# Attention and a feed-forward product on one core: row maximum and shift of the scores in one VectorE operation that works in place, and another order at the start

## The chip, the cores and the metric

One core of a Trainium2 chip runs the whole program. The metric is the device time of one execution in microseconds (us), given as the median over runs. TensorE (PE in the profile) does the matrix products and transposes, its weight loads are counted apart (PEld), VectorE is DVE, ScalarE is ACT, GpSimd is POOL, and SyncE (SP) issues every DMA.

## The reference

Queries, keys and values have 8 batches, 12 heads, 448 positions and 64 features. `g_q` and `g_k` are vectors of 64.

```
q_n, k_n = rmsnorm(q, g_q), rmsnorm(k, g_k)      # x / sqrt(mean(x*x) + 1e-6) * g
scores = q_n @ k_n.T / sqrt(64)
scores = scores - max(scores, axis=-1)
attn = exp(scores); attn = attn / (sum(attn, axis=-1) + 1e-9)
x = (attn @ v), heads side by side               # 3584 rows of 768
h = x @ w_in                                      # 768 x 2048
y = (h * cos(h)) @ w_out                          # 2048 x 768
```

The two weight matrices arrive as 64-bit floats.

## The kernel before

Two heads of one batch make a pair; there are 48 pairs, numbered u, six to a batch. The operands of the products are split into a rounded high part and a low rest (`hi` against `l` or `lo` in the names), and a product is summed up from passes over these parts.

What is done for a pair falls into two functions of the planner. `prepare(u)` loads the squares' input `sd`, squares it on ACT (L280), sums it on DVE (L283), and turns the sums into `r` = mean square to the power of -1/2 on POOL (`st_pow`, L291). `r` has 14 columns: 0 to 6 belong to the query rows, 7 to 13 to the key rows. The key factors go out to DRAM (`st_store`, L294) and come back spread over partitions as `rkb` (`rk_load`, L299); POOL multiplies the keys by them (`k_norm`, L309), ACT makes `khi` (L312) and POOL `kl` (L316). The queries are only multiplied by the gains (`q_scale`, L323), and split into `qhi` (L326) and `ql` (L330). The values are split on POOL (`v_high` L339, `v_low` L343).

`attend(u)` works on seven score tiles `S` of 128 query rows by 448 keys, each in one bank of PSUM; three such banks go round. `score` (L357) fills two tiles at a time, then one. `rowmax` (L363, one for each tile) takes the row maximum, `shift` (L368, one for each `score` call, so four for a pair) multiplies it by minus the query factor, and `expo` (L373) takes the exponential on ACT with the query factor as its scale and the shift as its bias, and sums the rows in the same pass. `sm` is the small tile of maxima, shifts and sums. The probabilities are transposed on TensorE four key blocks after another into one PSUM tile `PT` (L400), copied as `hi` on ACT (L407) and `lo` on DVE (L415, L417), and multiplied with the values into `O` (L427). The transposed row sums pass through the same tile (L402, once for a pair). After six pairs the batch is ready for the first product `ph` with `w_in` (L470 to L472), whose pieces stand between those of the next batches' attention. The weights `w_in` are decoded from 64 bits by four DVE operations (L208 to L216) and one on ACT (L214), split on ACT (L226) and POOL (L231). `w_out` goes the same way later. When all attention is done, a second part of the program does the cosine and the second product `y` (L541 to L543).

The order on every engine is set by a list scheduler at build time, `Plan`: each step is added with an engine, a cost in us, a due time, and the data that it reads and writes; at each free moment of an engine the step with the earliest due time among those that are ready is put next. `base(u)` is the due time of pair u, `SPLIT` the distance from the last pair of a batch to its first product. `SIGNAL` is added when a step waits for another engine, and `LEAD` on top of it when the waiting engine is TensorE. On the chip each engine then runs its list strictly in that order, and waits where the data is not there.

```
    SIGNAL = 0.16
    LEAD = 0.3
    ...
        return 30.0 + (PER0 * u if u < NP else PER0 * NP + PER * (u - NP))
```

Of the kernel before, what the change touches and what calls it, by code (L numbers as in the profile page):

```python
# [10 lines left out]
F32 = mybir.dt.float32  # L11
# [3 lines left out]
ALU = mybir.AluOpType  # L15
AX = mybir.AxisListType
# [11 lines left out]
class Plan:  # L28
# [9 lines left out]
    def __init__(self, rings):  # L38
        self.rings = rings
        self.parts = []  # L40
        self.start = []
        self.writer = {}
        self.readers = {}
        self.users = {}

    def add(self, eng, cost, due, fn, *args, r=(), w=(), land=0.0, start=0.0):
# [18 lines left out]
        self.start.append(start)  # L65

    def order(self):
# [21 lines left out]
        while True:  # L89
# [35 lines left out]
def tile_attention_moe(  # L125
# [11 lines left out]
    nc = tc.nc  # L137
# [4 lines left out]
    NVC = 5  # L142
    NCC = 6
# [38 lines left out]
    def g_fold():  # L182
# [7 lines left out]
        "sd": 1, "r": 5, "rkb": 1, "kd": 1, "kl": 2, "khi": 2, "qd": 1, "ql": 2, "qhi": 2, "vd": 1, "vs": 2, "S": 3, "sm": 3, "P": 12,  # L190
# [98 lines left out]
    def st_pow(u):  # L289
        r = pair[u]["r"]  # L290
        nc.gpsimd.tensor_tensor(r, r, nhalf.broadcast_to([128, 14]), ALU.pow)  # L291
# [52 lines left out]


    def score(u, j):
# [5 lines left out]
        for t in tiles:  # L352
            d["S", t] = ps_s.tile([128, 512], F32, tag="S", name=f"S{u}_{t}")
# [8 lines left out]
    def rowmax(u, t):  # L362
        nc.vector.reduce_max(pair[u]["sm"][:, 0, t : t + 1], pair[u]["S", t][:, :S], axis=AX.X)  # L363

    def shift(u, j):
        sm, r = pair[u]["sm"], pair[u]["r"]
        c = slice(3, 4) if j == 3 else slice(j, j + 5, 4)
        nc.vector.scalar_tensor_tensor(sm[:, 1, c], sm[:, 0, c], -1.0, r[:, c], op0=ALU.mult, op1=ALU.mult)  # L368

    def expo(u, t):  # L370
# [4 lines left out]
            bias=sm[:, 1, t : t + 1], scale=d["r"][:, t : t + 1], accum_out=sm[:, 2, t : t + 1],  # L375
# [187 lines left out]
    SPLIT = 56.0  # L563
# [3 lines left out]
    def base(u):  # L567
        return 30.0 + (PER0 * u if u < NP else PER0 * NP + PER * (u - NP))
# [33 lines left out]
    def prepare(u):  # L602
# [8 lines left out]
        add(POOL, 2.58, D0 - 34, st_pow, u, w=r)  # L611
        add(SP, ISS, D0 - 30, st_store, u, r=r, w=[("rkd", u)], land=LAND)
        add(SP, 2 * ISS, D0 - 26, rk_load, u, r=[("rkd", u)], w=[("rkb", u)], land=6.5)
# [3 lines left out]
        add(POOL, 0.8, D0 - 16, q_scale, u, r=[("gsc", 0)], w=qd)  # L617
        add(ACT, 0.6, D0 - 10, q_high, u, r=qd, w=qhi)
        add(POOL, 1.33, D0 - 8, q_low, u, r=qd + qhi, w=[("ql", u)])
        for hh in range(2):  # L620
            vd, vs = [("vd", 2 * u + hh)], [("vs", u, hh)]
            add(SP, ISS, D0 - 12 + 6 * hh, v_load, u, hh, w=vd, land=LAND)
            add(POOL, 0.56, D0 + 6 * hh, v_high, u, hh, r=vd, w=vs)
            add(POOL, 0.91, D0 + 2 + 6 * hh, v_low, u, hh, r=vd, w=vs)

    def attend(u):
        D0 = base(u)
        b, cc = divmod(u, NP)
        step = 4.0
        for j in range(4):  # L630
            tiles = (3,) if j == 3 else (j, j + 4)
            keys = [("S", 7 * u + 2 * j + n) for n in range(len(tiles))]
            dj = D0 + step * j
            add(PE, 0.88 if j < 3 else 0.62, dj, score, u, j,
                r=[("qhi", u), ("ql", u), ("khi", u), ("kl", u)], w=keys)
            for t, key in zip(tiles, keys):
                add(DVE, 0.61, dj + 1, rowmax, u, t, r=[key], w=[("sm", u, 0, t)])
            add(DVE, 0.25, dj + 1, shift, u, j, r=[("r", u)] + [("sm", u, 0, t) for t in tiles], w=[("sm", u, 1, j)])
            for n, (t, key) in enumerate(zip(tiles, keys)):
                add(ACT, 0.94, dj + 2, expo, u, t, r=[key, ("r", u), ("sm", u, 1, j)],  # L640
# [4 lines left out]
        for kc in range(4):  # L645
            dk = D1 + 4 * kc
            for hh, tiles in ((0, (0, 1, 2, 3)), (1, (4, 5, 6))):
# [8 lines left out]
                add(PE, 0.47 if hh == 0 else 0.36 + 0.11 * turn, dk, transp, u, kc, tiles, turn, r=r, w=w)  # L656
# [11 lines left out]
            for hh in range(2):  # L668
                n, m = 8 * u + 2 * kc + hh, 6 * u + 2 * kc + hh
                r = [[("hi", n), ("lo", m)], [("hi", n), ("lo", m)], [("lo", m)], [("hi", n), ("hi", n - 2)]][kc]  # L670
                add(PE, 0.21 if kc == 2 else 0.41, dk + 4, av, u, kc, hh, r=[("vs", u, hh)] + r, w=[("O", u, hh)])
# [126 lines left out]
```

## Time and profile before

| | us |
|---|---|
| median of 3 runs | 1604.09 |
| lowest and highest run | 1601.24 and 1608.01 |
| the profiled execution | 1605.41 |
| span of its profile | 1603.6 |
| busy: PE, PEld | 1483.6, 1250.6 |
| busy: DVE, ACT, POOL | 1081.9, 909.1, 880.9 |
| mean granted TensorE clock | 0.974 of full speed |

Busy times are sums over the span. What a stage is bound by is read from windows of the span, since the attention (from 30 us to some 1060 us) and the second product (the rest) have different limits. TensorE's matrix products overlap each other, so that one shows some 0.37 us where they start 0.20 us apart.

### The profile page before, as it was taken

The numbers are of one execution on the slowest core, as the hardware profiler recorded it, in microseconds if no ns is written. First come the engines' busy times: TensorE is split into PE (matmuls) and PEld (weight loads), VectorE is DVE, ScalarE is ACT, GpSimd is POOL, SyncE is SP. The second block draws the span as 40 slices with busy tenths as digits, with TensorE's granted clock in tenths as the row PEclk, the third lists the DMA queues.
The fourth block names the chain that finished last, engine by engine and source line by source line (L and its number), as shares of the span: only waits on it lengthen the run. The fifth ranks groups of instructions, "written<-read, shape, count | busy, mean of one in ns | idle before, by whom it ended". The sixth has DMA issues, their size and how long they took to land.

```text
span 1603.6 us, 22333 instructions
## 1 busy us (share of the span) xinstructions
PE 1483.6 (93%) x7680; PEld 1250.6 (78%) x7680; DVE 1081.9 (67%) x1723; ACT 909.1 (57%) x1786; POOL 880.9 (55%) x726
## 2 busy tenths in 40 slices
PE   0777889989999999999999999999999999999999
PEld 0455677778778877877777877879999999999998
DVE  5665899968777777787777776525266666666661
ACT  3556676667666677766677666634243444444432
POOL 7655767876475666576556564223245445444441
PEclk9877899999999999999999999999999999999999
DMA  5333662355445545545445543129422232322220
GB/s 168 106 91 117 193 212 92 110 149 166 147 148 158 160 145 163 158 132 161 133 136 168 152 148 92 54 83 353 138 92 69 93 104 60 102 92 81 81 81 35
DMA packets 118433, 205.24 MB, mean 128 GB/s; under 512 B 19680, under 2 KB 97840, under 8 KB 118320
## 3 DMA queue, kind: packets, MB, share of 16 engines
q1 hardware_dynamic: 118320, 203.82, 40.8%
q8 instruction: 60, 0.98, 0.3%
q14 instruction: 53, 0.43, 0.1%
HBM read 150.47 MB, written 53.30 MB: 127 GB/s over the span
## 4 chain that ended last, share of the span: by engine, by line
PE 60%; DVE 7%; ACT 4%; issue 2%; POOL 1%; DMA 0%; SPq 0%; ACTq 0%; POOLq 0%; DVEq 0%
PE y L541 10%; PE y L543 10%; PE y L542 10%; PE ph L470 6%; PE ph L471 6%; PE ph L472 6%; PE O L427 5%; PE PT L400 4%; PE S L357 4%; ACT hi L407 2%; DVE sm L363 1%; DVE lo L415 1%; ACT P L373 1%; DVE xf L442 1%; ACT xf L437 1%
## 5 line engine op out<-in xcount | busy, mean ns | idle before, releaser
L470 PE MATMUL ph<-xs,wi 128*128 128x448 f32 x768 | 300.5, 391 | 14.7 <-ACT he L482 14.7
L407 ACT CAST hi<-PT 128x448 fp32r<-128x448 f32 x384 | 187.9, 535 | 172.6 <-PE PT L400 72.5
L373 ACT ACTIVATE P<-S,sm,r 128x448 f32<-128x448 f32 x336 | 243.7, 732 | 73.8 <-DVE sm L368 72.7
L471 PE MATMUL ph<-xs,wi 128*128 128x448 f32 x768 | 284.0, 370 | 1.4 <-POOL xs L456 1.4
L472 PE MATMUL ph<-xs,wi 128*128 128x448 f32 x768 | 282.5, 368 | 0.0
L541 PE MATMUL y<-g,wo 128*128 128x448 f32 x768 | 281.1, 366 | 0.0
L542 PE MATMUL y<-g,wo 128*128 128x448 f32 x768 | 280.6, 365 | 0.0
L543 PE MATMUL y<-g,wo 128*128 128x448 f32 x768 | 280.6, 365 | 0.0
L525 POOL TENSOR_TENSOR g<-r,g 128x896 fp32r<-128x896 f32 x64 | 139.6, 2182 | 183.2 <-ACT g L527 183.2
L415 DVE TENSOR_TENSOR lo<-PT,hi 128x448 fp32r<-128x448 f32 x288 | 166.1, 616 | 95.4 <-ACT hi L407 91.9
L363 DVE TENSOR_REDUCE sm<-S 128x1 f32<-128x448 f32 x336 | 196.0, 613 | 43.1 <-PE S L357 42.3
L400 PE MATMUL PT<-ident,P 128*128 128x128 f32 x1344 | 194.0, 288 | 1.4 <-ACT P L373 1.4
L400 PEld LDWEIGHTS PT<-ident,P 128*128 128x128 f32 x1344 | 170.9, 150 | 20.5 <-issue 4.5
L470 PEld LDWEIGHTS ph<-xs,wi 128*128 128x128 f32 x768 | 146.3, 190 | 47.8 <-ACT he L482 19.8
L427 PE MATMUL O<-hi,vs 128*128 128x448 f32 x384 | 137.9, 410 | 21.6 <-ACT hi L407 7.0
L471 PEld LDWEIGHTS ph<-xs,wi 128*128 128x128 f32 x768 | 146.4, 191 | 13.1 <-POOL xs L456 4.2
L472 PEld LDWEIGHTS ph<-xs,wi 128*128 128x128 f32 x768 | 145.7, 190 | 12.5
L541 PEld LDWEIGHTS y<-g,wo 128*128 128x128 f32 x768 | 144.4, 188 | 12.7 <-ACT ye L551 0.7
L543 PEld LDWEIGHTS y<-g,wo 128*128 128x128 f32 x768 | 144.4, 188 | 11.3
L542 PEld LDWEIGHTS y<-g,wo 128*128 128x128 f32 x768 | 144.4, 188 | 11.1
L291 POOL TENSOR_TENSOR r<-r,nhalf 128x14 f32<-128x14 f32 x48 | 127.5, 2656 | 46.4 <-DVE r L287 38.3
L507 DVE TENSOR_TENSOR r<-hb,n 128x896 f32<-128x896 f32 x64 | 93.1, 1454 | 84.8 <-POOL g L525 81.7
(68 smaller groups left out, 2520.9 us busy)
## 6 DMA issues: line engine op xcount, KB each, us to landing
h_d<-he SPq DMA_DIRECT2D x128, 224.0 KB
hb<-h_d SPq DMA_DIRECT2D x64, 448.0 KB
sd<-sd SPq DMA_DIRECT2D x48, 448.0 KB
vd<-v SPq DMA_DIRECT2D x96, 160.0 KB
qd<-qT SPq DMA_DIRECT2D x48, 256.0 KB
raw<-w_in SPq DMA_DIRECT2D x16, 768.0 KB
rawo<-w_out SPq DMA_DIRECT2D x32, 384.0 KB
wo_d<-rawo SPq DMA_DIRECT2D x32, 384.0 KB
```

The lines of the kernel that those rows point to most:

```text
L363: nc.vector.reduce_max(pair[u]["sm"][:, 0, t : t + 1], pair[u]["S", t][:, :S], axis=AX.X)
L373: nc.scalar.activation(tl(u, f"P{t}", [128, S], F32, "P"), d.pop(("S", t))[:, :S], AF.Exp, bias=sm[:, 1, t : t + 1], scale=d["r"][:, t : t ...
L400: nc.tensor.transpose(pt[:, t * 128 : t * 128 + 128], src, ident)
L407: nc.scalar.copy(hi, pt[:, hh * S : hh * S + S])
L415: nc.vector.tensor_tensor(lo, src, hi.bitcast(F32), ALU.subtract)
L427: nc.tensor.matmul(O, st, d.pop((what, kb, hh)), start=(kc + n == 0), stop=(kc + n == 4))
L470: nc.tensor.matmul(ph[:, :S], whi, x2[:, 0, :], start=(cc == 0), stop=False)
L471: nc.tensor.matmul(ph[:, :S], whi, x2[:, 1, :], start=False, stop=False)
L472: nc.tensor.matmul(ph[:, :S], wlo, x2[:, 0, :], start=False, stop=(cc == NCC - 1))
L541: nc.tensor.matmul(y, whi, hi, start=(fc == 0), stop=False)
L542: nc.tensor.matmul(y, whi, lo, start=False, stop=False)
L543: nc.tensor.matmul(y, wlo, hi, start=False, stop=(fc == NFC - 1))
```

## The change

One VectorE operation, `rowmin`, takes the place of `rowmax` and `shift`: it multiplies a score tile in PSUM by minus the query factor, writes the product over the scores, and keeps the row minimum of what it wrote, which is the bias of the exponential. `expo` then has the constant -1 as its scale. Minus the query factor is a new small tile `nr`, made once for a pair by `st_negate`, a VectorE operation on 128x7 numbers. So each exponential waits for the operation on its own tile, and no longer for that on its neighbour.

For pair 0 `st_pow` is split: the seven key factors first, the seven query factors in a second operation, and `q_scale` and `v_high` of pair 0 are made to wait for the first. The due times are 8 us earlier (`base` begins at 22 instead of 30), `SPLIT` is 50 instead of 56, and `LEAD` is 0 for the TensorE steps of the first six pairs. The function `spare` has no effect, as `NSP` is 0.

```diff
-    def add(self, eng, cost, due, fn, *args, r=(), w=(), land=0.0, start=0.0):
+    def add(self, eng, cost, due, fn, *args, r=(), w=(), land=0.0, start=0.0, lead=None):
...
+        self.lead.append(self.LEAD * (eng == PE) if lead is None else lead)
...
-    def rowmax(u, t):
-        nc.vector.reduce_max(pair[u]["sm"][:, 0, t : t + 1], pair[u]["S", t][:, :S], axis=AX.X)
-
-    def shift(u, j):
-        sm, r = pair[u]["sm"], pair[u]["r"]
-        c = slice(3, 4) if j == 3 else slice(j, j + 5, 4)
-        nc.vector.scalar_tensor_tensor(sm[:, 1, c], sm[:, 0, c], -1.0, r[:, c], op0=ALU.mult, op1=ALU.mult)
+    def rowmin(u, t):
+        d = pair[u]
+        nc.vector.tensor_scalar(
+            d["S", t][:, :S], d["S", t][:, :S], d["nr"][:, t : t + 1], None, op0=ALU.mult, op1=ALU.min,
+            accum_out=d["sm"][:, 1, t : t + 1],
+        )
+
+    def st_negate(u):
+        nc.vector.tensor_scalar(
+            tl(u, "nr", [128, NQT], F32), pair[u]["r"][:, :NQT], -1.0, 0.0, op0=ALU.mult, op1=ALU.add
+        )
...
-            bias=sm[:, 1, t : t + 1], scale=d["r"][:, t : t + 1], accum_out=sm[:, 2, t : t + 1],
+            bias=sm[:, 1, t : t + 1], scale=-1.0, accum_out=sm[:, 2, t : t + 1],
...
-    SPLIT = 56.0
+    SPLIT = 50.0
...
-        return 30.0 + (PER0 * u if u < NP else PER0 * NP + PER * (u - NP))
+        return 22.0 + (PER0 * u if u < NP else PER0 * NP + PER * (u - NP))
...
-        add(POOL, 2.58, D0 - 34, st_pow, u, w=r)
+        rq = [("rq", u)]
+        if u:
+            add(POOL, 2.6, D0 - 34, st_pow, u, 0, 14, w=r + rq)
+        else:
+            add(POOL, 1.5, D0 - 34, st_pow, u, 7, 14, w=r)
...
+        if not u:
+            add(POOL, 1.5, D0 - 17, st_pow, u, 0, 7, r=r, w=rq)
...
+        add(DVE, 0.25, D0 - 10, st_negate, u, r=r + rq, w=[("nr", u)])
-        add(POOL, 0.8, D0 - 16, q_scale, u, r=[("gsc", 0)], w=qd)
+        add(POOL, 0.8, D0 - 16, q_scale, u, r=[("gsc", 0)] + ([] if u else r), w=qd)
...
-                add(DVE, 0.61, dj + 1, rowmax, u, t, r=[key], w=[("sm", u, 0, t)])
-            add(DVE, 0.25, dj + 1, shift, u, j, r=[("r", u)] + [("sm", u, 0, t) for t in tiles], w=[("sm", u, 1, j)])
+                add(DVE, 0.7, dj + 1, rowmin, u, t, r=[("nr", u)], w=[key, ("sm", u, 1, t)])
```

The order of the engines' lists moves with it. On POOL at the start, before, from the factors of pair 0 (`r0`) to the product of its keys (`kd0`); the digit behind a name is the pair, and `wi0` is the first block of `w_in`:

```order
L291 TENSOR_TENSOR r0_121<-r0_121,nhalf_94 128x14
L339 TENSOR_SCALAR vs0_117<-vd10_127 128x5x64
L343 TENSOR_TENSOR vs0_117<-vd10_127,vs0_117 128x5x64
L323 TENSOR_SCALAR qd1_134<-qd1_134,gs_93 128x512
L330 TENSOR_TENSOR ql1_158<-qd1_134,qhi1_152 128x512
L291 TENSOR_TENSOR r1_154<-r1_154,nhalf_94 128x14
L339 TENSOR_SCALAR vs1_172<-vd01_148 128x5x64
L343 TENSOR_TENSOR vs1_172<-vd01_148,vs1_172 128x5x64
L231 TENSOR_TENSOR wi0_156<-wf0_136,wi0_156 128x384 x2
L323 TENSOR_SCALAR qd2_168<-qd2_168,gs_93 128x512
L309 TENSOR_TENSOR kd0_103<-kd0_103,rkb0_160 128x448
```

Ahead of these rows POOL split the queries and half of the values of pair 0. The same place with the change, from POOL's first work of the kernel on (L294 is `st_pow`, L312 `k_norm`):

```order
L294 TENSOR_TENSOR r0_116<-r0_116,nhalf_94 128x7 x2
L326 TENSOR_SCALAR qd0_105<-qd0_105,gs_93 128x512
L342 TENSOR_SCALAR vs0_132<-vd00_108 128x5x64
L346 TENSOR_TENSOR vs0_132<-vd00_108,vs0_132 128x5x64
L333 TENSOR_TENSOR ql0_138<-qd0_105,qhi0_134 128x512
L234 TENSOR_TENSOR wi0_155<-wf0_126,wi0_155 128x384
L294 TENSOR_TENSOR r1_153<-r1_153,nhalf_94 128x14
L312 TENSOR_TENSOR kd0_103<-kd0_103,rkb0_142 128x448
```

The factors of pair 0 now stand first on POOL, and between them and the key product seven operations instead of ten, without the work of pairs 1 and 2 but for the factors of pair 1.

On ACT at the start, before, from the queries of pair 0 to its keys (`khi0`, L312):

```order
L326 CAST qhi0_119<-qd0_106 128x512
L214 ACTIVATE raw0_110<-raw0_110 128x768
L280 ACTIVATE sd1_129<-sd1_129 128x896
L326 CAST qhi1_152<-qd1_134 128x512
L226 CAST wi0_156<-wf0_136 128x768
L214 ACTIVATE raw1_114<-raw1_114 128x768
L226 CAST wi1_176<-wf1_144 128x768
L280 ACTIVATE sd2_165<-sd2_165 128x896
L312 CAST khi0_191<-kd0_103 128x448
```

With the change (`khi0` is L315):

```order
L329 CAST qhi0_134<-qd0_105 128x512
L217 ACTIVATE raw0_110<-raw0_110 128x768
L283 ACTIVATE sd1_119<-sd1_119 128x896
L229 CAST wi0_155<-wf0_126 128x768
L217 ACTIVATE raw1_113<-raw1_113 128x768
L229 CAST wi1_165<-wf1_145 128x768
L315 CAST khi0_172<-kd0_103 128x448
L329 CAST qhi1_175<-qd1_149 128x512
```

The queries of pair 1 and the squares of pair 2 have moved behind `khi0`; the decoding of two blocks of `w_in` still stands ahead of it.

On DVE, the first two groups of score tiles of pair 0, before:

```order
L363 TENSOR_REDUCE sm0_206<-S0_0_207 128x1
L363 TENSOR_REDUCE sm0_206<-S0_4_208 128x1
L368 SCALAR_TENSOR_TENSOR sm0_206<-sm0_206,r0_121 128x2
L363 TENSOR_REDUCE sm0_206<-S0_1_231 128x1
L363 TENSOR_REDUCE sm0_206<-S0_5_232 128x1
L368 SCALAR_TENSOR_TENSOR sm0_206<-sm0_206,r0_121 128x2
```

and with the change:

```order
L371 TENSOR_SCALAR S0_0_182,sm0_181<-S0_0_182,nr0_129 128x448
L371 TENSOR_SCALAR S0_4_183,sm0_181<-S0_4_183,nr0_129 128x448
L211 TENSOR_SCALAR wf2_212<-raw2_122 128x768
L213 SCALAR_TENSOR_TENSOR wf2_212<-raw2_122,wf2_212 128x768
L371 TENSOR_SCALAR S0_1_216,sm0_181<-S0_1_216,nr0_129 128x448
L371 TENSOR_SCALAR S0_5_217,sm0_181<-S0_5_217,nr0_129 128x448
```

The shift is gone, and the decoding of the third block of `w_in` begins between the two groups. On TensorE the number of instructions is the same; which piece of the first product stands between which pieces of the attention differs from pair to pair, and in pair 1 the score calls of its second and third group now stand behind each other, where products with the values of pair 0 stood between them.

More of the change, by code (lines that the diff above doesn't have):

```diff
@@ L112, in order @@
                 same = parts[m][0] == e and not land
-                gap = 0.0 if same else land + self.SIGNAL + self.LEAD * (parts[m][0] == PE)
+                gap = 0.0 if same else land + self.SIGNAL + self.lead[m]
                 ready[m] = max(ready[m], end + gap)
@@ L142, in tile_attention_moe @@
     NVC = 5
+    NSP = 0
     NCC = 6
@@ L189, in tile_attention_moe @@
     RING = {
-        "sd": 1, "r": 5, "rkb": 1, "kd": 1, "kl": 2, "khi": 2, "qd": 1, "ql": 2, "qhi": 2, "vd": 1, "vs": 2, "S": 3, "sm": 3, "P": 12,
+        "sd": 1, "r": 5, "rkb": 1, "kd": 1, "kl": 2, "khi": 2, "qd": 1, "ql": 2, "qhi": 2, "vd": 1, "vs": 2, "S": 3, "sm": 3, "nr": 3, "P": 12,
         "hi": 4, "lo": 2, "O": 1, "xf": 6, "rs": 1, "rt": 1, "ph": 1, "he": 2, "wf": 2,
@@ L287, in st_mean, with st_pow @@
         nc.vector.tensor_scalar(r, r, 1.0 / D, 1e-6, op0=ALU.mult, op1=ALU.add)
-    def st_pow(u):
-        r = pair[u]["r"]
-        nc.gpsimd.tensor_tensor(r, r, nhalf.broadcast_to([128, 14]), ALU.pow)
+    def st_pow(u, c0, c1):
+        r = pair[u]["r"][:, c0:c1]
+        nc.gpsimd.tensor_tensor(r, r, nhalf.broadcast_to([128, c1 - c0]), ALU.pow)
     def st_store(u):
@@ L629, in attend @@
         step = 4.0
+        lead = 0.0 if u < NP else None
         for j in range(4):
             tiles = (3,) if j == 3 else (j, j + 4)
-            keys = [("S", 7 * u + 2 * j + n) for n in range(len(tiles))]
+            keys = [("ph", u) if spare(u, t) else ("S", 7 * u + 2 * j + n - min(u, NSP)) for n, t in enumerate(tiles)]
             dj = D0 + step * j
-            add(PE, 0.88 if j < 3 else 0.62, dj, score, u, j,
+            add(PE, 0.88 if j < 3 else 0.62, dj, score, u, j, lead=lead,
                 r=[("qhi", u), ("ql", u), ("khi", u), ("kl", u)], w=keys)
             for t, key in zip(tiles, keys):
-                add(DVE, 0.61, dj + 1, rowmax, u, t, r=[key], w=[("sm", u, 0, t)])
-            add(DVE, 0.25, dj + 1, shift, u, j, r=[("r", u)] + [("sm", u, 0, t) for t in tiles], w=[("sm", u, 1, j)])
+                add(DVE, 0.7, dj + 1, rowmin, u, t, r=[("nr", u)], w=[key, ("sm", u, 1, t)])
             for n, (t, key) in enumerate(zip(tiles, keys)):
-                add(ACT, 0.94, dj + 2, expo, u, t, r=[key, ("r", u), ("sm", u, 1, j)],
+                add(ACT, 0.94, dj + 2, expo, u, t, r=[key, ("sm", u, 1, t)],
                     w=[("P", 7 * u + 2 * j + n), ("sm", u, 2, t)])
```

18 lines of the change are left out of this document (11 added, 7 removed).

## The prediction

> **What bounds the kernel now.** I read the busy shares in slices first, then windows cut at the stages, then the steps at which TensorE begins and passes from pair to pair, then the groups of the operations that the change touches, then the waits.
>
> ```profile
> PE   0777889989999999999999999999999999999999
> DVE  5665899968777777787777776525266666666661
> PEclk9877899999999999999999999999999999999999
> ```
>
> The program has an idle start, a stretch to about 180 us with TensorE at seven or eight tenths and a lowered clock, and then TensorE nearly full. The windows (busy us of PE, PEld, DVE, ACT, POOL, with counts, then the granted clock) say how full:
>
> ```profile
> 30.00:180.00 150.00, 111.43 (x448) 73.80 (x448) 97.27 (x190) 87.73 (x197) 90.76 (x81) 0.82 0.39 114
> 200.00:310.00 110.00, 100.82 (x540) 80.70 (x539) 103.48 (x168) 78.56 (x164) 82.68 (x66) 0.95 0.45 142
> 340.00:1060.00 720.00, 691.88 (x3847) 567.40 (x3848) 522.66 (x1003) 489.80 (x1096) 416.19 (x388) 1.00 0.46 141
> 1060.00:1604.00 544.00, 537.98 (x2645) 495.66 (x2643) 305.40 (x282) 208.24 (x243) 231.55 (x135) 1.00 0.32 106
> ```
>
> From 1060 us on TensorE is the bound and nothing that the change touches runs: that part costs the same. From 340 to 1060 it is idle for 28 us of 720. From 200 to 310 DVE is busy for 103.5 of 110 us (the blocks of `w_in` are decoded there), so DVE is the bound of that stretch. From 30 to 180 no engine is full: the pairs go by chains of short steps. How fast they go, the transposed row sums show, one for a pair (pairs 0, 6 and 47):
>
> ```profile
> 54.35 0.42 PE L402 MATMUL PT<-ident,sm 128*7 128x128 f32 x1
> 179.18 0.27 PE L402 MATMUL PT<-ident,sm 128*7 128x128 f32 x1
> 1048.19 0.27 PE L402 MATMUL PT<-ident,sm 128*7 128x128 f32 x1
> ```
>
> Six pairs in 124.8 us are 20.8 us each, and 41 pairs in 869 us are 21.2 us each, although the first six have hardly any of the first product beside them. So what is gained ahead of 180 us is latency, and it goes through to the end, since all behind it follows in order.
>
> **The start.** TensorE's first work is at 29.94 us:
>
> ```profile
> 6.55 0.17 DVE L287 TENSOR_SCALAR r<-r 128x14 f32<-128x14 f32 x1
> 7.53 0.69 POOL L323 TENSOR_SCALAR qd<-qd,gs 128x512 f32<-128x512 f32 x1 [6.24 <-DMA qd<-qT]
> 8.18 0.46 POOL L339 TENSOR_SCALAR vs<-vd 128x320 fp32r<-128x320 f32 x1
> 8.72 0.86 POOL L343 TENSOR_TENSOR vs<-vd,vs 128x320 fp32r<-128x320 f32 x1
> 9.63 1.58 DVE L208 TENSOR_SCALAR wf<-raw 128x768 int32<-128x768 int32 x1 [2.91 <-DMA raw<-w_in]
> 10.76 2.96 POOL L291 TENSOR_TENSOR r<-r,nhalf 128x14 f32<-128x14 f32 x1
> 13.75 0.33 SPq L294 DMA_DIRECT2D rk_d<-r  x1
> 14.58 1.20 DVE L216 SCALAR_TENSOR_TENSOR wf<-raw,wf 128x768 f32<-128x768 f32 x1
> 18.83 1.15 SPq L299 DMA_DIRECT2D rkb<-rk_d  x2
> 19.95 0.83 ACT L226 CAST wi<-wf 128x768 fp32r<-128x768 f32 x1
> 21.36 2.58 POOL L291 TENSOR_TENSOR r<-r,nhalf 128x14 f32<-128x14 f32 x1
> 25.27 1.95 POOL L231 TENSOR_TENSOR wi<-wf,wi 128x384 fp32r<-128x384 f32 x2
> 27.85 1.43 POOL L309 TENSOR_TENSOR kd<-kd,rkb 128x448 f32<-128x448 f32 x1
> 29.32 0.56 ACT L312 CAST khi<-kd 128x448 fp32r<-128x448 f32 x1 [4.22 <-POOL kd L309]
> 29.94 0.74 PE L357 MATMUL S<-khi,qhi 64*128 64x448 f32 x2 [29.94 <-ACT khi L312]
> ```
>
> The sums of pair 0 are ready at 6.7 us, but POOL takes their power only at 10.76; the store goes at 13.75 and the reload 5.1 us later; the key product waits to 27.85 behind other work on POOL. With the change the power of seven columns (about half of 2.6 to 3.0 us) runs from 6.7 to about 8.2, the store goes at 8.3 and the reload, by the same 5.1 us, at 13.4. SP has nothing ahead of that store but loads whose buffers are then free, and the second load of values, issued behind it, waits for POOL's `v_low` (second power 1.4, then 0.69, 0.46 and 0.86 behind 8.2: about 11.6), so the reload isn't held up. Then the key product is bound by POOL's list: the first piece of `wi0` and the power of pair 1 stand ahead of it. `wi0` follows the decoding: data at 9.63, the DVE operations to about 15.4 (15.8 before), the cast at 15.4 instead of 19.95, POOL's half (1.0) to 17.4, the power of pair 1 (2.6) to 20.0, the key product (1.3) to 21.3, `khi0` (0.56) and the first product at about 22. ACT's list allows it: the cast of the second block ends at about 20.5. **Term 1: -8 us.** Bounds: if both pieces ahead of the key product cost nothing, the reload's landing bounds it (13.4 plus some 4.5), so -12; if the squares of pair 1 or the second block of `w_in`, which ACT has ahead of `khi0`, arrive 4 us late, -4. The second power operation of pair 0 is hidden in POOL's wait for `wi0`.
>
> **The DVE operation.** What is removed:
>
> ```profile
> L363 DVE TENSOR_REDUCE sm<-S x336: 572/614/626, 34.8 to 1039.2; 128x1 f32<-128x448 f32 x168
> L368 DVE SCALAR_TENSOR_TENSOR sm<-sm,r x192: 139/165/1274, 36.0 to 1039.8; 128x2 f32<-128x2 f32 x144, 128x1 f32<-128x1 f32 x48
> L368 DVE SCALAR_TENSOR_TENSOR sm<-sm,r 128x2 f32<-128x2 f32 x144 | 56.9, 395 | 4.7
> L368 DVE SCALAR_TENSOR_TENSOR sm<-sm,r 128x1 f32<-128x1 f32 x48 | 13.6, 284 | 1.4
> L287 DVE TENSOR_SCALAR r<-r 128x14 f32<-128x14 f32 x48 | 13.0, 270 | 0.8
> L373 ACT ACTIVATION_READ_ACCUMULATOR P<-S,sm,r 128x1 f32 x336 | 68.6, 204 | 0.0
> ```
>
> The columns of the first two are ns, least, median and most. The maximum from PSUM is steady; the shift, of two numbers a row, has a median of 165 ns but a mean of 367 (70.5 us over 192), since it is often held to the end of a POOL operation. For a pair: 7 x 0.613 + 70.5/48 = 4.29 + 1.47 = 5.76 us.
>
> The new operation isn't in the trace. Its lower end is the maximum's own 0.613, the same tile read from PSUM; the upper end adds what ACT takes to read out its row sums, 0.204: 0.817. I take 0.70, nearer to the lower end, since DVE's smallest operations (the shift, 0.139 at the least) are shorter than ACT's read-out. `st_negate` is priced as L287, 0.27. For a pair 7 x 0.70 + 0.27 = 5.17, so 0.59 us of DVE less; at the ends 4.56 (-1.20) and 5.99 (+0.23). It breaks even at 0.784.
>
> The Trainium skill ("VectorE: DVE Perf Modes", section "Two Vector instructions with no wait between them") says that an operation which also writes out its accumulator is two instructions, the main one and a read of the accumulator. No DVE row here shows that; with ACT's row as its price the operation would stand at the upper end, and the sum below at about -8 instead of -22.
>
> The chain shortens besides. Before, ACT's first exponential of a group waited for two maxima and the shift; an example:
>
> ```profile
> 34.77 1.15 DVE L363 TENSOR_REDUCE sm<-S 128x1 f32<-128x448 f32 x2
> 35.91 0.86 POOL L343 TENSOR_TENSOR vs<-vd,vs 128x320 fp32r<-128x320 f32 x1
> 35.95 0.83 DVE L368 SCALAR_TENSOR_TENSOR sm<-sm,r 128x2 f32<-128x2 f32 x1
> 36.82 0.72 ACT L373 ACTIVATE P<-S,sm,r 128x448 f32<-128x448 f32 x1 [1.10 <-DVE sm L368]
> ```
>
> That is 2.05 us from the first maximum to the exponential (here the shift ended with POOL's operation); with the change it is one operation and a signal, about 0.75, or 0.6 to 1.3 us less. Which of it reaches the end, the waits tell (total us, times, longest; the last row is that pair of waits from 40 to 200 us alone):
>
> ```profile
> ACT P L373 <- DVE sm L368: 72.7, 60, 3.3
> PE O L427 <- DVE lo L415: 32.2, 37, 2.2
> PE ph L470 <- ACT he L482: 14.7, 11, 6.0
> PE S L357 <- ACT P L373: 12.7, 14, 4.5
> ACT P L373 <- DVE sm L368: 6.8, 8, 1.5
> ```
>
> ACT's 72.7 us are idle time of an engine that isn't the bound; TensorE waits for what stands behind, its 12.7 for a free score tile, 32.2 for `lo`, which DVE makes behind maxima and shifts, and 14.7 for ACT's copy of `ph`.
>
> **Term 2, pairs 0 to 6:** ACT's wait for shifts there is 6.8 us; it can go, but the transposes, `hi` and `lo` through the one PT tile are a second chain beside it. I take a bit over half, -4; bounds -8 (all of it and a little DVE time) and +3 (nothing of it, and the new order worse by 0.5 us a pair). **Term 3, 200 to 310 us:** DVE is the bound, 110/21.2 = 5.2 pairs at -0.59: -3; ends -6 and +1. **Term 4, 310 us to the end of the attention:** DVE is at 73% there, TensorE idle for 28 us; a quarter of that goes, since DVE has some 20 us less to do (34 pairs x 0.59) and ACT isn't held by shifts: -7. Bounds -15 (half) and +5 (the order, which differs in every pair, meets more late data). At ACT `expo` loses one operand and keeps its 0.73 us: nothing, ACT is busy for 71% at most in the stages above. POOL and the DMAs have the same work, apart from the split power.
>
> The sum: -8 - 4 - 3 - 7 = -22. The profiled execution took 1605.41 (span 1603.6), 1.3 above the median of the three runs; 1605.4 - 22 - 1.3 = **1582 us**. All ends together give 1563 and 1609; the likeliest case's own range is 1568 to 1592.
>
> **The rivals.** (a) Only the start counts: TensorE has 96% in the long stretch and the `lo` chain takes the rest as before. For it: ACT's waits for shifts are mostly beside TensorE's work. Then -8: 1596, just at the line of 0.5%. (b) Slower: the new operation takes 1.0 us or more, because it writes PSUM and hands out an accumulator, neither of which any DVE row shows. At 1.0 a pair has 7.27, +1.5 us; in the DVE-bound stretch that is +8 in full, in the other 42 pairs a third of it passes to TensorE (+21), less 8 at the start: 1624. It ends slower from about 0.9 on. Against it: the maxima, which read the same tiles, lie at 0.57 to 0.63 without exception. (c) TensorE's list holds: with `LEAD` 0, pair 1 has two score groups back to back, four tiles where three buffers go round, so the second group waits for an exponential, and products with values behind it wait too. If that costs one operation and one exponential (0.70 + 0.94) a pair for six pairs, +10, the start's gain is gone: 1602. Against: those products wait for `lo` anyway. (d) The first six pairs, freed of the shift, run at the planner's 16 us instead of 20.8: -29 in place of -4, 1557. For it: no engine is over 65% but TensorE, and that at a clock of 0.82. The Trainium skill ("TensorE: Matmul & The Clock Gate", part 1) says that a gate lets the full clock through only after a busy window of some 3.4 us; the 0.82 agrees with bursts and pauses, and by that rule a denser start would be clocked up and gain more. (e) That the change doesn't do what it says: the order shows both power operations of pair 0 side by side, so the queries are put off by one; this is in term 1.
>
> **How the numbers follow.** The forecast has 0.53, (a) 0.17, (b) 0.08, (c) 0.12, (d) 0.10. The range from 1557 to 1601 leaves out (b) and (c). A difference of 0.5%, 8 us, is about what a measurement of this kernel tells from none: faster (under 1596) are the forecast, (d) and a bit over half of (a): 0.73; the same are the rest of (a) and half of (c): 0.14; slower (b) and a part of (c): 0.13.
>
> **What would show it.** Term 1: the first L364 product at 20 to 24 us instead of 29.9. Term 2: the row sums of pair 6 pass TensorE 12 us earlier, at about 167. Term 3: DVE still full in its decoding stretch, which is shorter. Term 4: the wait of ACT for the shift is replaced by a smaller one for the new operation, and TensorE's 28 us shrink. The operation itself: 0.61 to 0.82, with or without a row for its accumulator. The prediction is wrong if that operation is over 0.9, if the start moves by less than 4 us, or if TensorE waits for score tiles (PE S behind ACT P) more than the 12.7 us of before.

## The result, and the profile after

The changed kernel takes 1559.4 us (median of 4 runs, 1559.26 to 1562.97) against 1602.66 for the kernel before on the same chip: a ratio of 0.973, 95% interval 0.970 to 0.975. That is 43 us, where 22 were forecast. The profiled execution took 1562.97, the slowest of the four, with a span of 1560.9. A few executions took far longer than the others of their kernel (two of five of e5_oldops, one of ten of e10_before_r10, and on two of the chips one of the kernel before), and the medians and ratios below leave them out.

The slices of the page, as before: the start is shorter, the clock in the first quarter higher.

```profile
PE   2777998899999999999999999999999999999999
DVE  6677999877877777777776675432566566666561
PEclk9898999999999999999999999999999999999999
```

Windows cut at the same stages (10 to 43 us earlier than before):

```profile
20.00:170.00 150.00, 110.27 (x496) 75.81 (x497) 107.86 (x242) 95.51 (x218) 108.35 (x97) 0.89 0.45 137
180.00:290.00 110.00, 100.39 (x545) 81.30 (x544) 103.87 (x189) 77.64 (x167) 86.27 (x70) 0.97 0.44 137
300.00:1017.00 717.00, 702.00 (x3933) 578.79 (x3932) 517.97 (x1156) 482.52 (x1120) 427.64 (x399) 1.00 0.47 145
1017.00:1561.00 544.00, 538.27 (x2614) 489.59 (x2612) 300.43 (x280) 207.79 (x241) 232.82 (x134) 1.00 0.32 105
```

DVE is as full as it was in the decoding stretch, and the second product is untouched. In the long stretch TensorE is idle for 15 us instead of 28, and does 3933 instructions in 717 us (5.49 a us) where it did 3847 in 720 (5.34).

Since the work moved ahead, these windows don't hold the same pieces of it. Cut where the row sums of a pair pass TensorE, they do but for a few instructions. From pair 0 to 6 and from pair 12 to 47, first before, then after:

```profile
54.35:179.18 124.83, 96.67 (x397) 64.55 (x396) 82.60 (x165) 74.32 (x168) 71.55 (x65) 0.78 0.39 114
308.11:1048.19 740.08, 706.98 (x3921) 579.45 (x3920) 541.65 (x1035) 506.75 (x1133) 439.96 (x409) 0.99 0.46 141
```

```profile
43.25:160.63 117.38, 88.10 (x403) 59.90 (x402) 82.67 (x192) 74.68 (x173) 79.64 (x73) 0.86 0.44 135
288.02:1000.71 712.69, 696.79 (x3910) 573.43 (x3908) 524.26 (x1170) 486.48 (x1131) 438.39 (x408) 1.00 0.48 147
```

From pair 12 to 47 TensorE's idle time fell from 33 to 16 us and its busy time by 10. From pair 0 to 6 it is idle for as long as before (28 and 29 us); what was gained there is all busy time, which fell by 8.6 us, at a granted clock of 0.86 instead of 0.78.

The transposed row sums of pairs 0, 6 and 47, and the first product of the program with what leads to it (L186 the gains, L294 the power, L297 the store, L302 the reload, L312 the key product):

```profile
43.25 0.42 PE L413 MATMUL PT<-ident,sm 128*7 128x128 f32 x1
160.63 0.38 PE L413 MATMUL PT<-ident,sm 128*7 128x128 f32 x1
1000.71 0.27 PE L413 MATMUL PT<-ident,sm 128*7 128x128 f32 x1
6.10 0.16 DVE L186 SCALAR_TENSOR_TENSOR gs<-gs 128x1 f32<-128x1 f32 x1 [5.22 <-DMA gs<-gg]
7.56 2.96 POOL L294 TENSOR_TENSOR r<-r,nhalf 128x7 f32<-128x7 f32 x2 [6.28 <-DVE r L290]
9.09 0.33 SPq L297 DMA_DIRECT2D rk_d<-r  x1
15.51 1.15 SPq L302 DMA_DIRECT2D rkb<-rk_d  x2
22.32 1.12 POOL L312 TENSOR_TENSOR kd<-kd,rkb 128x448 f32<-128x448 f32 x1
24.09 0.74 PE L364 MATMUL S<-khi,qhi 64*128 64x448 f32 x2 [24.09 <-ACT khi L315]
```

The operations (ns: least, median, most), and the first group of pair 0:

```profile
L371 DVE TENSOR_SCALAR_CACHE_REDUCE S<-S,nr x336: 641/684/694, 27.6 to 993.5; 128x448 f32<-128x448 f32 x168
L371 DVE DVE_READ_ACCUMULATOR S<-S,nr x336: 82/141/148, 28.2 to 994.1; 128x1 f32 x168
L377 DVE TENSOR_SCALAR nr<-r x48: 149/438/1237, 10.6 to 935.5; 128x7 f32<-128x7 f32 x48
L384 ACT ACTIVATE P<-S,sm x336: 610/638/680, 28.4 to 995.2; 128x448 f32<-128x448 f32 x168
...
27.65 0.68 DVE L371 TENSOR_SCALAR_CACHE_REDUCE S<-S,nr 128x448 f32<-128x448 f32 x1
28.25 0.13 DVE L371 DVE_READ_ACCUMULATOR S<-S,nr 128x1 f32 x1
28.25 0.68 DVE L371 TENSOR_SCALAR_CACHE_REDUCE S<-S,nr 128x448 f32<-128x448 f32 x1
28.42 0.63 ACT L384 ACTIVATE P<-S,sm 128x448 f32<-128x448 f32 x1 [2.80 <-DVE S L371]
28.85 0.14 DVE L371 DVE_READ_ACCUMULATOR S<-S,nr 128x1 f32 x1
```

The new operation does have a second instruction that reads its accumulator, but the next operation starts with that read, so operations of one group follow each other every 0.60 us. Before, two maxima took 1.15 us together and one 0.613, so that they followed every 0.53: by the same measure the new operation is longer by 0.07, not shorter. From its start to that of its exponential it is 0.77 us here, where 0.75 was forecast. The exponential has become shorter, 0.638 instead of 0.732 us, which was not forecast.

What waits (us in total, times, longest):

```profile
ACT P L384 <- DVE S L371: 87.1, 80, 2.8
PE O L438 <- DVE lo L426: 24.3, 30, 3.4
PE ph L481 <- ACT he L493: 3.5, 6, 1.1
PE S L364 <- ACT P L384: 11.9, 10, 2.4
```

ACT waits for DVE more than it did for the shift (72.7); TensorE waits less for `lo` (32.2), as little for score tiles (12.7), and only 3.5 us for ACT's copy of `ph`, where it was 14.7, the largest fall of the three. That fall alone isn't the gain: e10_before_r10 below has 6.5 us there and e3_plan 3.9, and the one is no faster than the kernel before, the other by 10 us.

### The profile page after: what moved, and what is told of

It is laid out like the page before. It is cut to its first block, busy times and chain, and to the rows that moved or that the text cites. A ratio compares the mean times of both kernels' runs of the same rounds, so it can differ in the third digit from the quotient of the medians.

```text
span 1560.9 us, 22589 instructions
## 1 busy us (share of the span) xinstructions
PE 1468.3 (94%) x7680; PEld 1239.3 (79%) x7680; DVE 1060.8 (68%) x1915; ACT 884.4 (57%) x1786; POOL 885.1 (57%) x727
## 4 chain that ended last, share of the span: by engine, by line
PE 73%; DVE 8%; ACT 2%; issue 2%; POOL 1%; DMA 1%; SPq 0%; ACTq 0%; POOLq 0%; DVEq 0%
PE y L554 10%; PE y L552 10%; PE y L553 10%; PE ph L481 8%; PE ph L482 7%; PE ph L483 7%; PE O L438 7%; PE PT L411 6%; PE S L364 6%; DVE lo L426 2%; ACT hi L418 1%; DVE S L371 1%; DVE xf L453 1%; DVE hi L428 1%; DVE wo L213 1%
## 5 line engine op out<-in xcount | busy, mean ns | idle before, releaser
L384 ACT ACTIVATE P<-S,sm 128x448 f32<-128x448 f32 x336 | 214.2, 641 | 97.9 <-DVE S L371 87.1
L371 DVE TENSOR_SCALAR_CACHE_REDUCE S<-S,nr 128x448 f32<-128x448 f32 x336 | 219.9, 683 | 30.4 <-PE S L364 26.0
L411 PE MATMUL PT<-ident,P 128*128 128x128 f32 x1344 | 186.9, 281 | 1.6 <-ACT P L384 1.6
L411 PEld LDWEIGHTS PT<-ident,P 128*128 128x128 f32 x1344 | 164.7, 145 | 18.5 <-issue 2.7
L483 PEld LDWEIGHTS ph<-xs,wi 128*128 128x128 f32 x768 | 145.2, 189 | 14.7 <-POOL wi L234 1.8
L482 PEld LDWEIGHTS ph<-xs,wi 128*128 128x128 f32 x768 | 145.7, 190 | 12.7 <-POOL xs L467 3.3
L438 PE MATMUL O<-hi,vs 128*128 128x448 f32 x384 | 133.0, 395 | 18.3 <-DVE xf L453 10.2
L529 DVE TENSOR_TENSOR r<-r,hb 128x896 f32<-128x896 f32 x64 | 73.9, 1154 | 108.5 <-ACT r L525 108.5
```

Source lines behind the costliest of these rows:

```text
L371: nc.vector.tensor_scalar(d["S", t][:, :S], d["S", t][:, :S], d["nr"][:, t : t + 1], None, op0=ALU.mult, op1=ALU.min, accum_out=d["sm"][:, ...
L384: nc.scalar.activation(tl(u, f"P{t}", [128, S], F32, "P"), d.pop(("S", t))[:, :S], AF.Exp, bias=sm[:, 1, t : t + 1], scale=-1.0, accum_out ...
L411: nc.tensor.transpose(pt[:, t * 128 : t * 128 + 128], src, ident)
L438: nc.tensor.matmul(O, st, d.pop((what, kb, hh)), start=(kc + n == 0), stop=(kc + n == 4))
L482: nc.tensor.matmul(ph[:, :S], whi, x2[:, 1, :], start=False, stop=False)
L483: nc.tensor.matmul(ph[:, :S], wlo, x2[:, 0, :], start=False, stop=(cc == NCC - 1))
```

## The experiments

The gain can be split along the program by the times at which the row sums of a pair pass TensorE, as in the rows above. All times are in us of one profiled execution each; "ratio" is that of the timed runs to the kernel before on the same chip, with its interval. Each column counts from the one before it, so that a row sums up to the span. "New" operations are the one with the minimum, the negation and the exponential with the constant.

| kernel | pair 0 passes | to pair 6 | to pair 12 | to pair 47 | rest of the span | ratio |
|---|---|---|---|---|---|---|
| before | 54.4 | 124.8 | 128.9 | 740.1 | 555.4 | 1 |
| changed | 43.2 | 117.4 | 127.4 | 712.7 | 560.2 | 0.973 (0.970 to 0.975) |
| e1_ops: new operations, list of before | 52.3 | 123.5 | 125.4 | 739.8 | 557.6 | 0.999 (0.997 to 1.001) |
| e3_plan: old operations, start and planner's numbers | 47.2 | 127.6 | 127.3 | 732.5 | 556.7 | 0.994 (0.992 to 0.996) |
| e4_opsplan: new operations, own list, old start | 53.8 | 109.3 | 120.6 | 731.3 | 558.4 | 0.985 (0.982 to 0.988) |
| e5_oldops: old operations, list of the changed one | 44.6 | 130.8 | 131.4 | 730.1 | 555.9 | 0.992 (0.989 to 0.994) |
| e8_group: changed, planned by groups | 48.7 | 113.9 | 123.4 | 714.3 | 556.1 | 0.970 (0.967 to 0.973) |
| e13_placeholder | 54.0 | 113.3 | 121.3 | 730.4 | 556.2 | 0.986 (0.982 to 0.990) |
| e14_noentry | 51.5 | 120.3 | 130.6 | 723.8 | 555.3 | 0.990 (0.987 to 0.994) |
| e15_earlynr | 53.9 | 118.9 | 127.6 | 734.2 | 555.3 | 0.994 (0.992 to 0.996) |
| e17_ops_cost70 | 54.3 | 116.9 | 127.1 | 740.5 | 559.5 | 0.995 (0.993 to 0.997) |

The rest of the span is the same in all to a few us.

**Operations or list?** The first four runs take the change apart.

e1_ops, the code of the new operations in the planning of before:

```diff
-    def rowmax(u, t): ...reduce_max...
+    def rowmax(u, t): (if t == 0: the negation) ...tensor_scalar mult, min, accum_out...
-    def shift(u, j): ...scalar_tensor_tensor...
+    def shift(u, j): pass
-            scale=d["r"][:, t : t + 1]
+            scale=-1.0
```

> The new operations in the list of before: every engine keeps the order of before, the maximum is replaced by the scaling with its minimum, the four shifts of a pair are left out, the negated factors are made right ahead of a pair's first tile, the exponential has the constant -1. Nothing of the start is changed. Theory A (the operations: the exponential went from 0.732 to 0.638 us, 0.66 us of ACT a pair, and the shift is gone from DVE): most of the gain beyond the start is here, -25 to -35, 1568 to 1578 us. Theory O (the order: new costs, due times and LEAD make a better list, the operations alone do little): -3 to -10, 1593 to 1600.

Measured: 1600.3, ratio 0.999, just past the upper end of theory O. Theory A fell: in this list the operations bring nothing that can be told. They are as short as in the changed kernel, here from the groups of lines (busy us, mean ns, idle before):

```profile
L368 DVE TENSOR_SCALAR_CACHE_REDUCE S<-S,nr 128x448 f32<-128x448 f32 x336 | 219.6, 686 | 50.4 <-PE S L357 41.2 <-ACT hi L413 3.8 <-DVE nr L365 0.2
L379 ACT ACTIVATE P<-S,sm 128x448 f32<-128x448 f32 x336 | 213.7, 644 | 37.6 <-DVE S L368 36.0 <-PE PT L406 0.4
```

and where their time went the waits tell, first those of before, then those of e1_ops:

```profile
ACT hi L407 <- PE PT L400: 72.5, 65, 4.3
ACT hi L407 <- PE PT L402: 45.9, 25, 4.2
```

```profile
ACT hi L413 <- PE PT L406: 100.7, 81, 4.4
ACT hi L413 <- PE PT L408: 70.2, 35, 4.7
ACT P L379 <- DVE S L368: 36.0, 32, 2.9
PE O L433 <- DVE lo L421: 32.2, 38, 2.5
PE ph L476 <- ACT he L488: 15.1, 10, 6.4
```

ACT waits 37 us less for DVE, and 52 us more for the transposes of TensorE. TensorE's own waits, 32.2 us for `lo` and 15.1 for ACT's copy of `ph`, are what they were (32.2 and 14.7). The time that was freed on ACT and DVE became waiting for TensorE, whose list stayed. The windows from 320 to 1000 us, of before, e1_ops, e4_opsplan and the changed kernel, show it as TensorE's instructions done in 680 us (the first count):

```profile
320.00:1000.00 680.00, 648.14 (x3593) 530.66 (x3591) 505.20 (x960) 469.64 (x1052) 418.91 (x388) 0.99 0.49 148
```

```profile
320.00:1000.00 680.00, 648.49 (x3599) 532.47 (x3600) 499.60 (x1095) 453.04 (x1055) 419.19 (x388) 0.99 0.49 147
```

```profile
320.00:1000.00 680.00, 659.81 (x3679) 542.34 (x3678) 503.91 (x1105) 459.67 (x1062) 414.28 (x385) 0.99 0.48 146
```

```profile
320.00:1000.00 680.00, 666.21 (x3747) 548.47 (x3746) 498.35 (x1115) 462.60 (x1077) 409.70 (x383) 1.00 0.47 146
```

e1_ops has ACT 17 us and DVE 6 us less busy than before, and TensorE does six instructions more. The kernels with a list of their own do 86 and 154 more.

e2_ap, the scale from a tile:

```diff
+    neg = cpool.tile([128, 1], F32, tag="neg", name="neg")
+    nc.vector.memset(neg, -1.0)
...
-            scale=-1.0
+            scale=neg
```

> The changed kernel, with the exponential's scale -1 read from a 128x1 tile instead of being a constant; order and all else are the same. If the operand is what made the exponential shorter, it shows 0.73 us again instead of 0.64. Theory A (ACT's shorter exponential is a good part of the gain): 10 to 20 us slower than the changed kernel, 1570 to 1580. Theory D (DVE's fusion and the finer waits are it, ACT had room): 0 to 4 us slower, 1559 to 1564. Theory O: the same, 1559 to 1563.

Measured: 1563.7, ratio 0.977 (0.974 to 0.980), 4 us from the changed kernel, with intervals that overlap. The exponential is at its old length again:

```profile
L386 ACT ACTIVATE P<-S,sm,neg 128x448 f32<-128x448 f32 x336 | 244.7, 732 | 91.8 <-DVE S L373 82.9 <-PE PT L413 5.9 <-DVE r L292 0.9
```

So the operand makes the difference of 0.09 us, and it is worth some 4 us of the 43 at this reading, which by the intervals could also be nothing: ACT has the room.

e3_plan leaves maximum, shift and exponential as they were and takes the rest of the change (the split power, `base`, `SPLIT`, `LEAD`, and the shorter landing times that the planner reckons with for the factors of pair 0); e4_opsplan does the opposite.

> The start and the planner's numbers alone: power of pair 0 in two halves, due times 8 us earlier, SPLIT 50, LEAD 0 for the first six pairs; maximum, shift and exponential as before, planned at their old costs. Theory O: most of the gain, -25 or more, below 1578. Theories A and D: the start only, -6 to -12, 1591 to 1597.

Measured: 1592.5, ratio 0.994, as theories A and D had it; theory O in its strong form, below 1578, fell. Pair 0 passes 7 us earlier, the first six pairs take 3 us longer, the long stretch 8 us less. These last 8 are of one execution, in which TensorE was idle there for 31 us, hardly less than the 33 of before, at a granted clock of 1.00 where it had been 0.99; a hundredth of 740 us is 7 us, so most of them may be the clock.

> The other half: the new operations with a list planned for them, but with due times, SPLIT, LEAD and the power of pair 0 as before. Theories A and D: -25 to -35, 1568 to 1578, and together with the start alone the two sum to the whole, -43. Theory O in the form that due times and LEAD matter: -5 to -12, 1591 to 1598.

Measured: 1578.6, ratio 0.985: 24 us. That is just outside theories A and D (1568 to 1578) and far from theory O's 1591 to 1598. The halves give 10 and 24 us, the whole 43: some 9 us come only with both, where each of the three has an interval of some 4 us to either side.

e5_oldops, the other cross: the list of the changed kernel, with a maximum and a shift of one column wherever the new operation stands.

```diff
-        nc.vector.tensor_scalar(d["S", t] ... op0=ALU.mult, op1=ALU.min, accum_out=...)
+        nc.vector.reduce_max(sm[:, 0, t : t + 1], pair[u]["S", t][:, :S], axis=AX.X)
+        nc.vector.scalar_tensor_tensor(sm[:, 1, t : t + 1], sm[:, 0, t : t + 1], -1.0, r[:, t : t + 1], ...)
```

> The list of the changed kernel with the operations of before in it: where the new operation stands, a maximum and a shift of its one column stand (336 shifts instead of 192, each some 0.3 us), the exponential has the query factor as its scale again and 0.73 us, the negation is left out, and the factors' tile has ten buffers instead of five, since it is read longer. DVE has about 1.2 us more a pair than in the changed kernel. Theory L (the list alone: the planner could place each exponential behind its own tile, and any operations do well in that order): 1560 to 1575. Theory B (list and operations need each other: the list is tight only for a DVE that has no shift): 1585 to 1605. Theory A (operations alone) has fallen with the first runs.

Measured: 1592.6, ratio 0.992, no better than with the old operations' own list and the same start. Theory L fell, theory B stands as far as this goes: the list of the changed kernel brings little to the old operations. But they are dearer here than before. In the groups of lines the shifts, 336 instead of 192, are still long and cost DVE 118 us instead of 70.5, so what this list would do with the four shifts of before isn't shown:

```profile
L371 DVE TENSOR_REDUCE sm<-S 128x1 f32<-128x448 f32 x336 | 205.9, 613 | 25.9 <-PE S L364 25.3
L372 DVE SCALAR_TENSOR_TENSOR sm<-sm,r 128x1 f32<-128x1 f32 x336 | 118.1, 351 | 12.0
```

**Is it the luck of the list?** Two kernels with one planned cost changed by 0.01 us, which reshuffles some thousands of rows.

```diff
-                add(DVE, 0.61, dj + 1, rowmax, ...        (e6_before62, from before: 0.62)
-                add(DVE, 0.7, dj + 1, rowmin, ...         (e7_after69, from the changed kernel: 0.69)
```

> The kernel before with one number of the planner changed, 0.62 instead of 0.61 as the cost of a maximum, so that the list is another one by chance and by nothing else. Theory R (much of the gain is the luck of the list): 10 us or more away from 1603, either way. Theories L and B: within 6 us of 1603, 1597 to 1609.

> The changed kernel with 0.69 instead of 0.70 as the planner's cost of the new operation: another list by chance. Theory R: 1570 to 1590. Theories L and B: within 6 us of the changed kernel, 1553 to 1566.

Measured: 1604.1, ratio 0.999 (0.997 to 1.001), and 1561.4, ratio 0.973 (0.970 to 0.975). In these two tries luck is worth 2 us at most; theory R fell. (The cost of 0.80 in e18_after80, below, gave 1568.3 us, so that a larger step can move a list by some more.)

**What makes a list suit the operations?** Tried in turn: the finer wait (e8), the longer freedom of the buffers of `r` (e9 to e11), the shift's entry (e13, e14), the place of the negation (e15), planned costs (e16 to e18).

```diff
-                add(ACT, 0.94, dj + 2, expo, u, t, r=[key, ("sm", u, 1, t)],
+                add(ACT, 0.94, dj + 2, expo, u, t, r=[key] + [("sm", u, 1, x) for x in tiles],   (e8_group)
+                add(ACT, 0.94, dj + 2, expo, u, t, r=[key, ("r", u), ("sm", u, 1, t)],           (e9_rheld)
```

> The changed kernel, planned as if an exponential waited for the operations on both tiles of its score group, as it did before; the operations are the changed ones. Theory F (the finer wait, tile by tile, is what the list gains by): 1575 to 1590. If the gain is DVE's shorter work or the lack of the shift: 1557 to 1566.

Measured: 1558.0, ratio 0.970, not to be told from the changed kernel. Theory F fell.

> The changed kernel, planned as if the exponential still read the factors' tile r. In the list of before the five buffers of r are held until a pair's last exponential, so the squares of pair u+5 or 6 are the furthest that DVE's list goes ahead; in the changed one r is free after the negation, and the list goes up to 9 pairs ahead. This kernel has the changed operations and again at most 6 pairs ahead. Theory G (the list gains because r is free earlier, a side of the change that nothing says): 1572 to 1590. Theory H (how far ahead is of no matter, the list gains because it was made for the new operations' costs): 1555 to 1564.

Measured: 1561.1, ratio 0.976 (0.972 to 0.979), as theory H had it.

```diff
-        "sd": 1, "r": 5,      (e10_before_r10 in before, e11_ops_r10 in e1_ops)
+        "sd": 1, "r": 10,
```

> The kernel before with ten buffers for r instead of five, in the planner and on the chip; its list then goes up to 11 pairs ahead. Theory G: faster than before by 10 to 25, 1578 to 1593. Theory G with B (the freedom is of use only to the new operations): 1597 to 1605. Theory H: the same as before, 1599 to 1608.

> The new operations in the list of before, as in the first run, but that list made with ten buffers for r; nothing of the start. Theory G: what the first run lacked, so 1572 to 1585, like the run with the operations and their own list (1579). Theory H: as the first run, 1595 to 1605.

Measured: 1603.6, ratio 1.000 (0.998 to 1.001), and 1606.8, ratio 1.002 (1.000 to 1.004). Theory G fell on all three.

> An attempt at a better version: the changed kernel, planned for exponentials behind their whole group (it was 1558), with ten buffers for r and eight for the negated factors, so that the list may go up to 15 pairs ahead. Theory G, if more freedom still pays: 1545 to 1556. Theory H, or if nine pairs ahead are enough: 1555 to 1563.

Measured: 1570.6, ratio 0.979 (0.977 to 0.981): slower than e8_group, from which it differs by the buffers alone. More freedom to run ahead did harm here, which neither theory had expected; the long stretch took 723.5 us instead of 714.3.

The next three change the planning between e1_ops and e4_opsplan step by step. In e13 the exponentials wait for the entry, in e14 for both operations of their group, and in e15 every operation waits for the negation.

```diff
+            add(DVE, 0.25, dj + 1, nothing, r=[("sm", u, 1, t) for t in tiles], w=[("sh", u, j)])   (e13, in e4_opsplan)
-            add(DVE, 0.25, dj + 1, shift, ...)                                                      (e14, in e1_ops)
+        add(DVE, 0.25, D0 - 10, st_negate, u, r=r, w=[("nr", u)])                                   (e15, in e1_ops)
```

> The new operations with their own list and nothing of the start (1579 before), but planned with an entry of 0.25 us on DVE between a group's two operations and its exponentials, as the shift was; the entry emits no instruction. Theory S (the shift's entry in the planning is what spoils the list): 1595 to 1605. Theory C (the operation's cost, 0.70 against 0.61, is it): 1572 to 1585.

Measured: 1581.5, ratio 0.986. The entry doesn't spoil a good planning: theory S fell in its plain form.

> The new operations planned like before (cost 0.61, exponential behind both operations of its group, negation ahead of the first tile), but without the shift's entry in the planning. Theory S: 1572 to 1585, the list has what it lacked. Theory C: 1595 to 1605, as in the list of before (1600).

Measured: 1587.7, ratio 0.990. Without the entry the bad planning gains 0.8% over e1_ops, more than half of the way to e4_opsplan; it lies between what the two theories expected.

> The new operations planned like before with the shift's empty entry, and the negation as a step of its own well ahead of its pair, as in the changed kernel, instead of right ahead of the first tile, where it takes DVE 0.49 us on the way to every pair's first exponential. If that place is what the operations lost in the list of before: 1575 to 1588. Theories S and C: 1594 to 1605.

Measured: 1594.1, ratio 0.994. The place of the negation alone gains 0.5% over e1_ops, less than was expected if it were the cause.

```diff
-            add(DVE, 0.25, dj + 1, shift, ...      (e16_before_shift45, in before: 0.45)
-                add(DVE, 0.61, dj + 1, rowmax, ... (e17_ops_cost70, in e1_ops: 0.70)
-                add(DVE, 0.7, dj + 1, rowmin, ...  (e18_after80, in the changed kernel: 0.80)
```

> The kernel before, planned with 0.45 us for a shift instead of 0.25; it took 0.37 on average. Theory C (lists planned with costs under the measured ones are bad ones): 1580 to 1595. If planned costs of that size matter only for the new operations: 1599 to 1608.

Measured: 1605.0, ratio 1.001 (0.998 to 1.003). The kernel before did not suffer from its planned shift.

> The first run (new operations in the planning of before, with the shift's empty entry and the negation ahead of the first tile, 1600) with 0.70 instead of 0.61 as the planned cost of the operation. Theory C: 1578 to 1590. If neither cost nor place nor entry is a cause by itself: 1593 to 1603.

Measured: 1598.3, ratio 0.995 (0.993 to 0.997), 0.3% better than e1_ops, with intervals that overlap.

> The changed kernel with 0.80 instead of 0.70 as the planned cost, near what lies between the operation's start and that of its exponential. Theory C, if the higher cost still pays: 1545 to 1556. If 0.70 is enough: 1556 to 1566.

Measured: 1568.3, ratio 0.977 (0.974 to 0.980): no faster than with 0.70, and slower than either range. The intervals overlap, so that it is slower isn't sure. Theory C fell too, as a cause by itself.

So no one number of the planning is the cause. With the new operations, moving the negation (0.5%), leaving out the entry (0.8%) and perhaps the cost (0.3%) each improved the list of before a little, where 1.4% lie between e1_ops and e4_opsplan. They don't simply add up: e13 has the entry and is as good as e4_opsplan without it. Which rows of the list these move, and why the old operations gain from none of what was tried on their list, stays open.

## Why the prediction was half right

The direction and the mechanism at the start were right, and 1559 lies within the range; the gain was twice what was forecast, and nearly all that is missing is in term 4. By the terms:

**Term 1, the start (-8).** The first product came at 24.09 instead of 29.94, -6, within its bounds. The power found POOL free, as worked out, and took 1.5 us for each half, but it began at 7.56 instead of 6.7: DVE's work on the gains waited for their load to 6.10 (5.35 before), and the sums of pair 0 stand behind it. The reload went 6.4 us behind the store instead of 5.1, since it waited for the store to land. That cost nothing, since the key product waited for POOL's list, as worked out. The decoding was later than reckoned (its second DVE operation, L213, took 1.38 and 1.91 us, where L210 had 0.96), and with it the factors of pair 1, at 19.1 to 22.3 instead of 17.4 to 20.0. By the passing of pair 0 the gain was 11 us, and most of it is there with the old operations: 7 in e3_plan, 10 in e5_oldops. The prediction says that such a gain goes through to the end. With the new operations that isn't borne out: e4_opsplan and e13_placeholder, with the start of before, let pair 12 pass at 283.7 and 288.6 us, the changed kernel at 288.0.

**The operation's price (0.70).** A median of 0.684 and a read of 0.14, overlapped: 0.60 from start to start. So rival (b) fell, and so did the upper end. The Trainium skill's rule ("VectorE: DVE Perf Modes", "Two Vector instructions with no wait between them") that an operation with an accumulator is two instructions is borne out by the L371 rows; that the second would cost as much as ACT's (0.204) is not. `st_negate` took 0.49 on average instead of 0.27. For a pair that is 7 x 0.60 + 0.49 = 4.69 us. The 5.76 of before counts the maxima by their length; by their step of 0.53 it is 7 x 0.53 + 1.47 = 5.18. So DVE has 0.49 us a pair less, near the forecast of 0.59, and its busy time from pair 12 to 47 agrees: 541.65 - 524.26 = 17.4 us over 35 pairs, 0.50 for each. The exponential was put at nothing, as if it kept its 0.73 us; it fell to 0.638, which e2_ap puts at some 4 us of the time.

**Term 2, the first six pairs (-4).** -7.4, within its bounds, but not by the way that was worked out. ACT's wait for shifts was to go. From 54 to 180 us it was 4.9 us before, and from 43 to 161 us with the change it is 3.8, now for the new operation:

```profile
ACT P L373 <- DVE sm L368: 4.9, 6, 1.5
ACT P L384 <- DVE S L371: 3.8, 4, 1.4
```

TensorE's idle time there didn't fall at all; its busy time did, at the higher clock. So the size came out by luck. That the new operations matter there holds: in lists planned for them these pairs take 109 to 120 us in all runs, with the old operations in any list 123 to 131, and with the new ones in the list of before 123 and 126 (e1_ops, e11_ops_r10). Through which wait they do so stays open.

**Term 3, the decoding stretch (-3).** From pair 6 to 12, -1.5; DVE is still full there, 103.87 of 110.

**Term 4, the rest of the attention (-7): the step that failed.** From pair 12 to 47 it is 740.1 - 712.7 = 27 us, beyond the lower bound of -15. Two errors are in that step.

The first is that the new due times and `SPLIT` were priced at nothing behind the start, as an order that differs by chance. By chance that stretch moved by 3 and 4 us (e6 and e7: 742.8 and 708.9). With the new operations and a list of their own, but the numbers of before, it takes 731.3 us (e4_opsplan) and 730.4 (e13_placeholder), some -9, about what was forecast for the operations. With the numbers of the change it takes 712.7 and, planned by groups, 714.3 (e8_group): 16 to 19 us more are gained. The margins are smaller when every list is counted, since e14_noentry has 723.8 with the numbers of before, and e12_group_r10 and e18_after80 have 723.5 and 723.6 with those of the change. With the old operations the same numbers bring 8 in a list of their own (e3_plan) and 10 in that of the changed kernel (e5_oldops), and the new operations in the list of before bring nothing (739.8, e1_ops). So the 27 take both. Of the numbers, only `base` and `SPLIT` are set for steps behind the first six pairs; which of the two it is, and why it needs the new operations, no run shows.

The second is that the size was read as a quarter of TensorE's 28 us of idle time. From pair 12 to 47 the idle time was 33 us, and half of it went, 17 us. The other 10 came out of its busy time: it does 12 instructions less there, which at 707/3920 = 0.18 us each is some 2 us, and the granted clock rose from 0.990 to 0.998 (0.99 and 1.00 in the rows), which on 707 us is some 6 us. These two are estimates from the windows and the trace's clock; one execution of each kernel was profiled.

**Rivals.** (a) fell with the result, though it describes e3_plan well (1592.5 for 1596). (c) fell as a price: TensorE's waits for score tiles are 11.9 us, not above the 12.7 of before. Its mechanism shows a little, since from pair 0 to 6 that wait rose from 1.7 to 5.0 us. (Its sum was off besides: +10 on the forecast's own terms gives 1592; 1602 leaves out terms 3 and 4.) (d) fell: the first six pairs take 19.6 us each, not 16. What (d) expected of the clock did come, 0.86 instead of 0.78 from pair 0 to 6. Its sum, 1557, is nearest to the measured time by luck, for the time was gained elsewhere.

## What to carry to other kernels

In this kernel, whose engines follow a fixed list, a shorter operation off the bound engine gave nothing as long as the list stayed: the freed time turned into waits for the engine that is the bound (e1_ops). Price such a change together with a list planned for it, and treat the planner's due times as a part of the change: with the new operations they were worth 16 to 19 us in the long stretch between the nearest kernels, with the old ones 8 to 10. A fraction of TensorE's idle time is a poor measure of what a better order can gain; here half of it went, and the busy time fell besides. And a gain at the start need not reach the end: cut the program at later points too, and see whether it is still there.

## What had not been expected of the hardware

The exponential from PSUM on 448 columns takes 0.732 us with its scale in a 128x1 tile and 0.638 with a constant (the bias is a tile in both); e2_ap brought the 0.732 back. On DVE the read of an accumulator (0.14) runs beside the next operation's start, and operations that read and overwrite the same PSUM tile and keep its minimum follow every 0.60 us, against 0.53 for the maximum alone (1.15 us for two, 0.613 for one). Price an operation by the step at which it repeats, not by the length that its row shows. Small VectorE operations from SBUF stay uneven: the negation of 128x7 numbers took from 0.149 to 1.237 us.
